# One order for two plans, later index copies and products of ones in an attention and expert kernel

## The chip, the cores and the metric

The kernel runs on one core of a Trainium2 chip. The metric is the time of one execution on the device in microseconds (us), as the median of the timed runs. A profile is one more execution, with its own time.

## The reference

Attention without a softmax, normalised per head, and then a mixture of experts with one expert per token:

```
kv  = einsum('bhsd,bhse->bhde', k, v)          # 8 batches, 8 heads, 576 tokens, 64
out = einsum('bhsd,bhde->bhse', q, kv)
x   = out / sqrt(mean(out*out) + 1e-6) * g_norm    # to [4608, 512]
e   = argmax(x @ w_gate);  p = softmax probability of e
# each of 8 experts keeps its first 1152 tokens, in order
y   = relu(x_e @ w1[e]) @ w2[e]                # 512 -> 1024 -> 512
result[token] = p * y   (0 for a token that was not kept)
```

All inputs are float32. The kernel splits float32 operands of the expert products into a high and a low float16 part and adds three products (high by high, high by low, low by high).

## The kernel before

**Attention.** Eight batches, each loaded in halves of four heads (k, v, q), through rings of three buffers that SyncE's queue fills. Of a batch, TensorE multiplies k by v, turns q (transposes by an identity, `turn` in `unit`, line 793) and multiplies turned q by kv (`product`, 818). VectorE and ScalarE copy results, make squares, a reciprocal root and the logits. `route` (866) makes of the logits the chosen expert, and of counts (products with a triangle of ones, L991) each token's place with its expert. `enter` (1028) adds ten small products per batch into one PSUM tile, `tab`: the table of tokens by expert and slot, complete after the last batch. The normalised rows go to a DRAM buffer `x_dram` from GpSimd's queue (L1050, L1052).

**Early expert.** After batch 2 the expert with the most tokens so far is picked, its weights are loaded and split, and after batch 4 its first 384 tokens are gathered and worked on within the attention part: first products in PSUM tiles named `op`, and the first of three row tiles of the second products also in `op`.

**Tables.** `finish` (1304) is the end of the first plan: it reads `tab` (L1112), cuts the row indices of the early expert's remaining rows, and ranks the experts (L1072 to L1108).

**Rounds.** The rest of the early expert (its row tiles 1 and 2 in PSUM tiles named `yp`; the rows from 384 to 704: round 0), then seven experts in order of their counts, with 672 to 544 rows each. For each round: weights are loaded in quarters (L341), VectorE takes maxima (`am`, L357), a scale is made through two small TensorE products (L370, L377) and a chain of small VectorE operations (`scale`, 379), ScalarE makes the high part (L391) and VectorE the low part (L397, tiles `w1l` and `w2l`). Rows are gathered by GpSimd (`xg`, L453), multiplied by the norm (`xm`), split and turned. Round 0's three row tiles are turned by TensorE (L472); later rounds' by transposing DMAs. First products are at L557 (`hp`), second ones at L604 and L613 (`yp`).

**Index copies.** `slots` (663) reads an expert's place in the table into a register and copies six columns of two tables (L669): a register load and two small copies. `rows_beside` (1588) calls it for each of the seven later rounds, and the gathers of that round use the copy. Its only dependency is the ranking.

**What sets the order.** A `Plan` (90) holds every step with its engines, an assumed length, dependencies and a key. `place` puts steps on engines by those lengths, the one that can start first, and among several that can start, the smallest key; no actual time enters. `emit` then writes out all steps by planned start. There are two plans: the first for attention, early expert and `finish`, the second for the rest. Each is written out within a region of its own, `tc.manual_schedule`, in which an engine keeps the order in which its instructions were written. Between the regions the pools of the attention part are closed.

Of the kernel before, what the change touches and what calls it, by code (L numbers as in the profile page):

```python
# [26 lines left out]
MANUAL = ("PE", "Activation", "DVE", "Pool", "SP")  # L27
# [17 lines left out]
FIRST = -50.0  # L45
KEY = 10.0
EARLY_TILES = 1
ROWS = 0.0
# [13 lines left out]
ON_X = 0  # L62

TARDY = (3.0, 3.0, 3.0, 3.0, 1.5, 3.0, 2.0, 0.5)
LATE = (4.0, 2.0, 1.0, 2.0)


# [22 lines left out]
class Plan:  # L90
# [5 lines left out]
    def op(self, ways, fn, deps=(), key=0.0, takes=(), uses=()):  # L96

        ways = [ways] if isinstance(ways[0], str) else list(ways)
        o = Op(ways, fn, [d for d in deps if d is not None], list(takes), key)
        for h in takes + uses if isinstance(takes, tuple) and isinstance(uses, tuple) else list(takes) + list(uses):  # L100
            h.users.append(o)
        self.ops.append(o)
        return o
# [56 lines left out]
def attention_moe_kernel(  # L160
# [12 lines left out]
    nc = tc.nc  # L173
# [4 lines left out]
    P = 128  # L178
# [507 lines left out]
    nc.vector.memset(warm, 0.0)  # L686
    nc.scalar.activation(warm, warm, AF.Exp)

    o_sbs, sss = [], []
    for i in range(NO):  # L690
        o_sbs.append(at.tile([P, C, H, XW], F32, name=f"o_sb{i}", bufs=1))
# [3 lines left out]
    op = plan.op  # L695
# [97 lines left out]
    def unit(b, n, ts, kv, ready, oh):  # L793
        key = b * C + n * C / len(UNITS)
        o_sb, kv2 = oh.t, kv.t.rearrange("p h f x -> p (h f) x")
        qp, qt = new("qp"), new("qt")
        half, u = UNITS[n]
        qh, qd = ts["q", half]
        m = 2 * len(BLOCKS[u]) * P

        def turn(e):
            qp.t = bank("qp")
            for w, t in enumerate(BLOCKS[u]):
                for p in range(2):
                    nc.tensor.transpose(qp.t[:, (2 * w + p) * P:(2 * w + p + 1) * P],
                                        qh.flat[:, (t + C * p) * P:(t + C * p + 1) * P], ident)

        def keep(e):
            qt.t = at.tile([P, 512], F32, name="qt", bufs=3)
            copy(e, qt.t[:, 0:m], qp.t[:, 0:m])  # L810

        o = op(("T", m / 980), turn, [qd], key - 1.2, (qp,), (qh,))
        kept = op([("A", 0.48), ("V", 0.6)] if m == 512 else [("A", 0.29), ("V", 0.34)], keep, [o], key - 1, (qt,), (qp,))
        done = []
        for w, t in enumerate(BLOCKS[u]):
            ph = new("op")

            def product(e, w=w, t=t, ph=ph):
                ph.t = bank("op")
                for p in range(2):  # L820
                    f = 2 * (half * HH + 2 * p + (t > 2))
                    x = kv2[:, f:f + 4:3] if t == 2 else kv2[:, f:f + 2]
                    nc.tensor.matmul(ph.t[:, p * 2 * XW:(p + 1) * 2 * XW], lhsT=qt.t[:, (2 * w + p) * P:(2 * w + p + 1) * P],  # L823
                                     rhs=x, start=True, stop=True)

            o = op(("T", 0.55), product, [kept] + ready, key, (ph,), (qt, kv))
            for s0, s1 in ((0, 1), (1, 2)) if t == 2 else ((0, 2),):

                def out_(e, t=t, ph=ph, s0=s0, s1=s1):
                    m0 = 2 * t + s0  # L830
                    h0, c0 = half * HH + m0 // C, m0 % C
                    copy(e, o_sb[:, c0:c0 + s1 - s0, h0:h0 + 3:2].rearrange("p c h x -> p h c x"),
                         ph.t[:, 0:4 * XW].rearrange("p (h c x) -> p h c x", h=2, c=2)[:, :, s0:s1])

                a = op([("A", 0.29), ("V", 0.37)] if s1 - s0 == 2 else [("A", 0.2), ("V", 0.22)], out_, [o], key, (oh,), (ph,))
                done += [((2 * t + i) % C, a) for i in range(s0, s1)]
        return done
# [28 lines left out]
    def route(b, oh, ssh, outs, sums):  # L866
# [159 lines left out]
                                 in1=tok_hl[:, :, cs].rearrange("p i (o c) -> p i o c", o=1).broadcast_to(s4), op=ALU.mult)  # L1026

        def enter(e):
            for c in range(C):
                for i in range(2):  # L1030
                    nc.tensor.matmul(tab[:, 0:W], lhsT=z["ohl"][:, :, c], rhs=z["rhs"][:, i, :, c],
                                     start=(b == 0 and c == 0 and i == 0), stop=(b == NB - 1 and c == C - 1 and i == 1),
                                     skip_group_check=True)
# [84 lines left out]
    def early_weights():  # L1118

        cnt = sm.tile([P, E], F32, name="cnt")  # L1120
        o = count(cnt, (PICK_AFTER + 1) * C)
        o = op(("V", 1.7), lambda e: pick(cnt), [o], (PICK_AFTER + 1) * C)

        def reg(e):
            early["reg"] = nc.sync.value_load(first_i[0:1, 0:1], min_val=0, max_val=E - 1)

        early["picked"] = [o]
        reg = op(("S", 0.05), reg, [o], W1_KEY)
        free = [[], [], [], []]
        for i, key in ((0, W1_KEY), (1, W2_KEY)):  # L1130
            loads = [op(("S", 0.43), lambda e, i=i, p=p: load_weight(i, early["reg"], raw1, p, 4),
                        [reg] + free[p], key) for p in range(4)]
            waits.append((loads, WAFTER[i]))
            loads = [op(("D", 1.46), None, [o]) for o in loads]
            for o in loads:
                o.late = LATE[3]
            f, z = split_weight(i, wsets[0], raw1)
            tops = []
            for p in range(4):
                key = WKEYS[i][0] + 2 * p * WKEYS[i][1]  # L1140
                if TOPS[i][p] == "A":
                    tops += [op(("A", 0.63), lambda e, f=f, p=p: f["sum"](p), [loads[p // 2]], key)
                             for p in (2 * p, 2 * p + 1)]
                else:
                    tops += [op(("V", 0.61), lambda e, f=f, p=p: f["top"](p), [loads[p // 2]], key)
                             for p in (2 * p, 2 * p + 1)]
            key = WKEYS[i][0] + 8 * WKEYS[i][1]
            o = op(("V", 0.3), lambda e, f=f: f["most"](), tops, key)
            o = op(("T", 0.12), lambda e, f=f: f["across"](misc[:, 128:256]), [o], FIRST)
            o = op(("V", 0.2), lambda e, f=f: f["across_max"](misc[:, 128:256]), [o], FIRST)  # L1150
            o = op(("T", 0.35), lambda e, f=f: f["back"](misc[:, 96:97]), [o], FIRST)
            o = op(("V", 1.1), lambda e, f=f: f["scale"](misc[:, 96:97]), [o], FIRST)
            free, highs, lows = [list(tops[2 * p:2 * p + 2]) for p in range(4)], {}, {}
            for n, p in enumerate((0, 2, 4, 6, 1, 3, 5, 7) if i == 0 else range(8)):
                after = key + n * WKEYS[i][1]
                highs[p] = a = op(HIGHS, lambda e, f=f, p=p: f["high"](p, e), [o], after)
                lows[p] = c = op(LOWS, lambda e, f=f, p=p: f["low"](p, e), [a], after)
                free[p // 2] += [a, c]
            early["free"] = free
            early["w", i], early["z", i] = (highs, lows), z  # L1160
# [180 lines left out]
    order = ExitStack()  # L1341
    order.enter_context(tc.manual_schedule(engines={getattr(mybir.EngineType, e) for e in MANUAL}))
    plan.emit()
    order.close()
    actx.close()


# [187 lines left out]
    def weights(r, key, after):  # L1535

        ws, sets, zs, holds = wsets[r % 2], [], [], []
        for i in range(2):
# [35 lines left out]
            o.late = LATE[2] if r > 1 else 0.0  # L1574
            o = op(("T", 0.31), lambda e, f=f, x=x: f["back"](x.t[:, 0:1]), [o], FIRST, (), (x,))
            ew = new(f"e{i}")
            o = op(("V", 1.1), lambda e, f=f, x=x: f["scale"](x.t[:, 0:1]), [o], FIRST, (ew,), (x,))
            zs.append((z, o, ew))
            highs, lows = [], []
            for p in range(8):  # L1580
# [4 lines left out]
            holds.append(hold)  # L1585
        return sets, zs, holds

    def rows_beside(r, key):

        hold, sl, st = new("xs"), new("slots"), {}  # L1590

        def cut(e):
            st["gi"], st["si"] = slots(mo, perm_i[0:1, 1, r:r + 1])

        cut_ = op(("V", 0.4), cut, [early["rank"]], key, (sl,))
        n = len(spans(0, BUDGET[r]))
        gates, turned, first, sent = [], [], None, []
        for i in range(n):
# [23 lines left out]
    def products(r, x, xh, xl, gates, xs_hold, si, sl_hold, sets, zs, w_holds, s0, s1):  # L1622
# [32 lines left out]
        def scales(e):  # L1655
            st["g2"] = Gemm2(mo, wsets[r % 2], st["g1"], x().gt, si(), s0, s1)
            st["g2"].scales(y_scale(*[z["e"] for z, _, _ in zs]))

        scaled = op(("V", 1.2), scales, hh[:1] + gates + [o for _, o, _ in zs], urgent, (),
                    (xs_hold, *[x for _, _, x in zs]))  # L1660
        second(r, st, hh, hl, sets and sets[1], scaled, hid, w_holds[1], sl_hold, s0, s1, y_bank)
        return hh
# [5 lines left out]
    def moved(e):  # L1668
# [6 lines left out]
                                              mo, None, lambda: psx.tile([P, 512], F32, tag="x", name="xp"), new("xs"), BM)  # L1675
    args = (lambda st=st: st["rows"], xh, xl, gates, xs_hold, lambda: early["si0"], Hold(None), None, zs, w_holds, EARLY,
            BUDGET[0])
    for r in range(E):
        hh = products(r, *args)
        key = KEY * r  # L1680
        if r + 1 < E:
            sets, zs, w_holds = weights(r + 1, key + 1, [] if r > 1 else sent)
            st, xs_hold, sl, gates, turned, sent = rows_beside(r + 1, key + ROWS)
            args = (lambda st=st: st["x"], turned, turned, gates, xs_hold, lambda st=st: st["si"], sl, sets, zs, w_holds, 0,
                    BUDGET[r + 1])
        else:
            op(("P", 9.0), lambda e: nc.gpsimd.drain(), hh[:2], key)
            steps, o = plan_rest(), hh[0]
            for _ in range(60):
                o = op(("V", 0.2), lambda e: next(steps, None), [o], key + 1)  # L1690
    order = ExitStack()
    order.enter_context(tc.manual_schedule(engines={getattr(mybir.EngineType, e) for e in MANUAL}))
    plan.emit()
    order.close()
    rest(**table)
# [31 lines left out]
```

## Time and profile before

| | |
|---|---|
| timed runs, median of 3 | 574.98 us (573.97 to 575.07) |
| profiled execution | 569.37 us |
| its span, first to last instruction | 567.6 us |
| TensorE (PE) busy | 528.5 us, 93% of the span |
| VectorE (DVE) busy | 386.8 us, 68% |
| ScalarE (ACT) busy | 252.6 us, 45% |
| GpSimd (POOL) busy | 198.9 us, 35% |
| mean granted TensorE clock | 0.982 of 2.4 GHz |

An instruction's row has its start in us from the span's start, its length, engine, line, operation, written tile <- read tiles, shapes, the count of merged instructions, and in brackets the idle time of its engine just before it with what ended that. "issue" is idle time for which the profile shows no releaser. PEld is TensorE's weight load. The granted clock is a share of 2.4 GHz: 1.00 is that level, 0.50 is 1.2 GHz.

### The profile page before, as it was taken

Reading aid. Unit: us, or ns where it says so; the run is one execution under the profiler, and the core shown is the slowest. Engines: PE = TensorE matmul, PEld = TensorE weight load, DVE = VectorE, ACT = ScalarE, POOL = GpSimd, SP = SyncE. Lnnn points to the kernel's source line nnn. Section 1 sums busy time; section 2 is a strip of 40 time slices with the busy share of each in tenths; the row PEclk is TensorE's granted clock in tenths of the full one; section 3 lists DMA queues with packets and bytes.
Section 4 is the critical chain, followed back from the end, with each engine's and each line's share of the span. In section 5 each row is a group of like instructions: output and inputs, shape, how many; then the busy total and the mean of one; then the engine's idle time right before and its main releaser. Section 6 shows DMA issues by size and latency. Waiting matters only on the chain.

```text
span 567.6 us, 11867 instructions
## 1 busy us (share of the span) xinstructions
PE 528.5 (93%) x4490; PEld 364.6 (64%) x4490; DVE 386.8 (68%) x1072; ACT 252.6 (45%) x490; POOL 198.9 (35%) x244
## 2 busy tenths in 40 slices
PE   4999987978877999999999999999999999999995
PEld 4988876965434576546754674677477558648843
DVE  4387897999838999998999677395848607203800
ACT  1687663886102662655625524253353426212201
POOL 3003335245132471355506431742452375021011
PEclk9999995999999999999999999999999999999998
DMA  8999999662149589699667565583665342010000
GB/s 279 332 357 357 377 383 381 210 257 95 52 150 360 113 250 261 154 308 180 198 160 239 163 153 164 143 172 101 206 159 122 79 102 57 18 55 22 2 37 33
DMA packets 81905, 102.71 MB, mean 181 GB/s; under 512 B 39148, under 2 KB 63724, under 8 KB 80818
## 3 DMA queue, kind: packets, MB, share of 16 engines
q1 hardware_dynamic: 74240, 70.50, 43.3%
q0 software_dynamic: 7584, 31.38, 16.7%
q8 instruction: 37, 0.61, 0.4%
q14 instruction: 26, 0.21, 0.1%
q10 hardware_dynamic: 18, 0.02, 0.0%
HBM read 73.20 MB, written 20.68 MB: 165 GB/s over the span
## 4 chain that ended last, share of the span: by engine, by line
issue 32%; PE 29%; DMA 16%; POOL 13%; DVE 8%; ACT 1%; POOLq 1%; SPq 0%; DVEq 0%
PE hp L557 10%; PE yp L604 9%; DMA v_sb<-in_v_dram 4%; POOL out_dram L634 4%; DMA k_sb<-in_k_dram 4%; POOL pair L490 4%; DMA q_sb<-in_q_dram 3%; POOL xg L453 3%; PE op L823 2%; POOL xm L461 2%; DMA xs<-pair 2%; DVE w1l L397 2%; PE op L557 2%; DMA raw<-in_moe_w_dram 2%; DMA xg<-x_dram,gi 1%
## 5 line engine op out<-in xcount | busy, mean ns | idle before, releaser
L557 PE MATMUL hp<-xs,w1h 128*128 128x320 f16 (+6 forms) x960 | 134.2, 292 | 2.4 <-DVE gt L466 1.2
L557 PEld LDWEIGHTS <-w1h 128*128 128x128 f16 x1024 | 99.4, 98 | 40.0 <-issue 7.3
L634 POOL DMA_INDIRECT out_dram<-ysb,si x42 | 42.9, 1020 | 153.8 <-ACT ysb L629 150.7
L604 PEld LDWEIGHTS <-hh 128*128 128x128 f16 x560 | 54.4, 98 | 63.7 <-issue 1.6
L562 ACT ACTIVATE hh<-hp 128x320 f16<-128x320 f32 (+7 forms) x64 | 41.0, 640 | 108.5 <-PE hp L557 108.5
L357 DVE TENSOR_REDUCE am<-raw 128x1 f32<-128x512 f32 x120 | 75.6, 673 | 4.1 <-DMA raw<-in_moe_w_dram 4.1
L629 ACT ACTIVATE ysb<-yp,ysc 128x512 f32<-128x512 f32 (+5 forms) x41 | 28.1, 685 | 99.9 <-PE yp L604 93.6
L557 PE MATMUL hp<-xs,w1l 128*128 128x320 f16 (+6 forms) x480 | 72.0, 292 | 0.0
L565 DVE SCALAR_TENSOR_TENSOR hl<-hp,hh 128x320 f16<-128x320 f32 (+7 forms) x64 | 47.4, 741 | 32.8 <-ACT hh L562 32.7
L604 PE MATMUL yp<-w2h,hh 128*128 128x512 f16 x272 | 65.3, 379 | 0.8 <-ACT ysb L629 0.8
L604 PE MATMUL yp<-w2l,hh 128*128 128x512 f16 x272 | 65.4, 383 | 0.0
L604 PE MATMUL yp<-w2h,hl 128*128 128x512 f16 x272 | 65.0, 381 | 0.0
L453 POOL DMA_INDIRECT xg<-x_dram,gi x42 | 44.0, 1048 | 49.6 <-DVE gt L466 13.0
L557 PEld LDWEIGHTS <-w1l 128*128 128x128 f16 x512 | 49.8, 98 | 16.3
L823 PE MATMUL op<-kv_bd,qt 128*128 128x144 f32 x320 | 53.0, 301 | 3.5 <-ACT qt L703 2.7
L397 DVE SCALAR_TENSOR_TENSOR w2l<-raw,sw,w2h 128x512 f16<-128x512 f32 x64 | 51.6, 848 | 5.2 <-ACT w2h L391 5.2
L619 DVE COPY yt<-yp 128x256 f32<-128x256 f32 (+4 forms) x7 | 2.9, 412 | 73.4 <-PE yp L613 63.8
L490 POOL TENSOR_TENSOR pair<-xm,pair 128x512 f16<-128x512 f32 (+5 forms) x26 | 34.0, 1308 | 50.3 <-ACT pair L486 50.1
L397 DVE SCALAR_TENSOR_TENSOR w1l<-raw,sg,w1h 128x512 f16<-128x512 f32 x64 | 50.1, 816 | 1.5 <-ACT w1h L391 1.5
L604 PEld LDWEIGHTS <-hl 128*128 128x128 f16 x280 | 27.3, 98 | 32.2 <-issue 1.1
L823 PEld LDWEIGHTS op<-kv_bd,qt 128*128 128x128 f32 x320 | 44.1, 196 | 5.6 <-ACT qt L703 2.9
L391 ACT ACTIVATE w2h<-raw,sw 128x512 f16<-128x512 f32 x62 | 39.7, 710 | 8.1 <-PE yp L613 7.2
(247 smaller groups left out, 698.0 us busy)
## 6 DMA issues: line engine op xcount, KB each, us to landing
raw<-in_moe_w_dram SPq DMA_DIRECT2D x64, 512.0 KB, 5.4
x_dram<-o_sb POOLq DMA_DIRECT2D x8, 720.0 KB, 6.5
k_sb<-in_k_dram SPq DMA_DIRECT2D x16, 320.0 KB, 6.6
v_sb<-in_v_dram SPq DMA_DIRECT2D x16, 320.0 KB, 7.9
q_sb<-in_q_dram SPq DMA_DIRECT2D x16, 320.0 KB, 6.9
x_dram<-o_sb POOLq DMA_DIRECT2D x8, 576.0 KB, 7.4
k_sb<-in_k_dram SPq DMA_DIRECT2D x16, 256.0 KB
v_sb<-in_v_dram SPq DMA_DIRECT2D x16, 256.0 KB, 4.5
```

The costliest lines, as they stand in the source:

```text
L357: nc.vector.tensor_reduce(out=am()[:, p:p + 1], in_=raw[:, sl(p)], axis=AX.X, op=ALU.max, apply_absolute_value=True)
L391: nc.scalar.activation(wh[:, sl(p)], raw[:, sl(p)], AF.Copy, scale=z["s"])
L397: nc.vector.scalar_tensor_tensor(out=wl[:, sl(p)], in0=raw[:, sl(p)], scalar=z["s"], in1=wh[:, sl(p)], op0=ALU.mult, op1=ALU.subtract)
L453: nc.gpsimd.indirect_dma_start(out=self.xg[i][0:n], out_offset=None, in_=x_dram[0:self.rows, :], in_offset=bass.IndirectOffsetOnAxis(ap=se ...
L490: eng.tensor_tensor(out=pair[0:n, 1], in0=self.xm[i][0:n], in1=pair[0:n, 0], op=ALU.subtract)
L557: nc.tensor.matmul(self.view(hp)[:, v], lhsT=w[:, c, f * P:(f + 1) * P], rhs=x[:, c, u * hw:(u + 1) * hw], start=(t == 0 and c == 0), stop ...
L562: nc.scalar.activation(self.out(self.hh, j), self.view(hp), AF.Relu)
L565: nc.vector.scalar_tensor_tensor(out=self.out(self.hl, j), in0=self.view(hp), scalar=0.0, in1=self.out(self.hh, j), op0=ALU.max, op1=ALU.s ...
L604: nc.tensor.matmul(yp[0:n, 0:DM], lhsT=h[:, j, o:o + n], rhs=w[:, j, :], start=(m == 0), stop=(m == len(self.terms) - 1))
L629: nc.scalar.activation(self.ysb[0:n], yp[0:n, 0:DM], AF.Copy, scale=self.ysc[0:n, i:i + 1])
L634: nc.gpsimd.indirect_dma_start(out=(disjoint.pop() if disjoint else out)[:, :], out_offset=bass.IndirectOffsetOnAxis(ap=self.sidx[0:n, col ...
L823: nc.tensor.matmul(ph.t[:, p * 2 * XW:(p + 1) * 2 * XW], lhsT=qt.t[:, (2 * w + p) * P:(2 * w + p + 1) * P], rhs=x, start=True, stop=True)
```

## The change

A helper `busy` issues products of a matrix of ones with itself, 256 columns each, into an unused part of the PSUM tile `misc`; their results are not read. It is called ahead of one turn of batch 3 (6 products), one of batch 4 (24), both the first turn of q's second half, and ahead of the first product of batch 7 (10). The other places where it could be called have zero. The planned lengths don't count it.

The first region is no longer closed after the first plan: both plans are written out in one. In the second plan, index copies for the rounds from the second on also depend on the last low part of round 0's rows. Three assumed lengths grow: an index copy from 0.4 to 0.9, `scale` from 1.1 to 1.4 in weights of the rounds from the second on, and `scales` (the output scale) from 1.2 to 2.4 in the rounds from the first on.

```diff
+BUSY_TURNS = {(3, 1): 0.7, (4, 1): 2.6}
+BUSY_PRODUCTS = {(7, 0, 0): 1.1}
+BUSY_ENTERS = {}
+BUSY_SCALES = (0.0, 0.0)
...
+    def busy(us, dst=None):
+        dst = misc if dst is None else dst
+        for _ in range(round(us / 0.109)):
+            nc.tensor.matmul(dst[:, 256:512], lhsT=ones16, rhs=ones16.rearrange("p (o x) -> p o x", o=1).broadcast_to([P, 2, P]),
+                             start=True, stop=True)
...
         def turn(e):
+            busy(BUSY_TURNS.get((b, n), 0.0))
             qp.t = bank("qp")
...
             def product(e, w=w, t=t, ph=ph):
+                busy(BUSY_PRODUCTS.get((b, n, w), 0.0))
                 ph.t = bank("op")
...
     plan.emit()
-    order.close()
     actx.close()
...
-            o = op(("V", 1.1), lambda e, f=f, x=x: f["scale"](x.t[:, 0:1]), [o], FIRST, (ew,), (x,))
+            o = op(("V", 1.4 if r > 1 else 1.1), lambda e, f=f, x=x: f["scale"](x.t[:, 0:1]), [o], FIRST, (ew,), (x,))
...
-    def rows_beside(r, key):
+    def rows_beside(r, key, after=()):
...
-        cut_ = op(("V", 0.4), cut, [early["rank"]], key, (sl,))
+        cut_ = op(("V", 0.9), cut, [early["rank"], *after], key, (sl,))
...
-        scaled = op(("V", 1.2), scales, hh[:1] + gates + [o for _, o, _ in zs], urgent, (),
+        scaled = op(("V", 2.4 if r > 0 else 1.2), scales, hh[:1] + gates + [o for _, o, _ in zs], urgent, (),
...
+    placed = xl[-1:]
     for r in range(E):
...
-            st, xs_hold, sl, gates, turned, sent = rows_beside(r + 1, key + ROWS)
+            st, xs_hold, sl, gates, turned, sent = rows_beside(r + 1, key + ROWS, placed if r else ())
...
-    order = ExitStack()
-    order.enter_context(tc.manual_schedule(engines={getattr(mybir.EngineType, e) for e in MANUAL}))
     plan.emit()
     order.close()
```

## Rows read from the trace of the kernel before

**Rows 1.** The page's part 1: engine, busy us, share of the span, instructions.
```profile
PE 528.5 (93%) x4490; PEld 364.6 (64%) x4490; DVE 386.8 (68%) x1072; ACT 252.6 (45%) x490; POOL 198.9 (35%) x244
```

**Rows 2.** Waits of PE from 185 us on: total us, times, longest.
```profile
PE hp L557 <- DVE gt L466: 1.2, 1, 1.2
```

**Rows 3.** Sums by stretch: length, busy PE PEld DVE ACT POOL, clock, DMA share, GB/s.
```profile
92.70:99.60 6.90, 6.82 (x47) 6.74 (x48) 3.69 (x15) 4.24 (x10) 4.13 (x4) 0.51 1.10 374
98.00:150.00 52.00, 45.06 (x410) 35.55 (x409) 50.20 (x159) 36.26 (x91) 18.20 (x26) 0.99 0.46 164
154.50:176.50 22.00, 14.36 (x72) 7.16 (x71) 10.05 (x42) 3.61 (x6) 7.79 (x8) 0.92 0.65 229
158.50:159.00 0.50, 0.50 (x4) 0.21 (x3) 0.00 (x0) 0.00 (x0) 0.00 (x0) 1.00 0.06 25
167.70:171.20 3.50, 3.47 (x11) 1.79 (x12) 1.69 (x9) 0.59 (x1) 1.17 (x2) 0.51 0.91 267
176.50:204.50 28.00, 27.57 (x244) 17.35 (x244) 27.16 (x73) 16.76 (x31) 13.73 (x13) 1.00 0.70 199
```

**Rows 4.** Timeline of PE, then of DVE, around the join of the plans.
```profile
155.32 1.89 PE L604 MATMUL yp<-w2h,hh 128*128 128x512 f16 x8 [0.78 <-ACT ysb L629]
159.85 0.75 PE L1031 MATMUL tab<-rhs,ohl 128*128 128x48 f16 x10
...
155.39 0.46 DVE L1024 TENSOR_TENSOR rhs<-ohh,tok_hl 128x480 f16<-128x480 f16 x1
160.63 0.27 DVE L1112 SCALAR_TENSOR_TENSOR tab_sb<-slot_pos,cap,tab 128x48 f32<-128x48 f32 x1 [4.78 <-PE tab L1031]
166.93 0.69 DVE L461 TENSOR_TENSOR xm<-xg 128x512 f32<-128x512 f32 x1 [2.29 <-issue]
167.54 0.26 DVE L1108 TENSOR_REDUCE bud_e<-cmp 128x8 f32<-128x64 f32 x1
```

**Rows 5.** The chain that ended last: start, us, what.
```profile
165.65 6.38 DMA xg<-x_dram,gi
...
174.83 0.68 DVE xm L461
```

**Rows 6.** Timeline of DVE from the second tile on, and PE's first product.
```profile
168.69 0.17 DVE L669 COPY gi<-gidx_tab 128x6 int32 x1 [0.60 <-issue]
...
172.06 0.15 DVE L466 TENSOR_SCALAR gt<-xg 64x1 f32<-64x1 f32 x1 [0.27 <-DMA xg<-x_dram,gi]
172.82 0.17 DVE L669 COPY gi<-gidx_tab 128x6 int32 x1 [0.62 <-issue]
...
174.61 0.17 DVE L669 COPY gi<-gidx_tab 128x6 int32 x1 [0.60 <-issue]
...
176.48 1.76 PE L557 MATMUL hp<-xs,w1h 128*128 128x320 f16 x11 [0.46 <-ACT xs L703]
```

**Rows 7.** Timeline of POOL and SP: the first gather, and round 1's weights.
```profile
163.06 1.03 POOL L453 DMA_INDIRECT xg<-x_dram,gi  x1 [6.27 <-DVE cmp L1096]
164.93 5.97 SPq L341 DMA_DIRECT2D raw<-in_moe_w_dram  x8
```

**Rows 8.** Timeline: DVE's last low part of round 1's w1, PE's first use.
```profile
204.16 0.73 DVE L397 SCALAR_TENSOR_TENSOR w1l<-raw,sg,w1h 128x512 f16<-128x512 f32 x1
206.86 1.30 PE L557 MATMUL hp<-xs,w1l 128*128 128x336 f16 x8
```

**Rows 9.** Timeline of PE and DVE in the attention part.
```profile
70.31 0.66 PE L805 MATMUL qp<-ident,q_sb 128*128 128x128 f32 x4
86.50 2.40 PE L739 MATMUL a<-v_sb,k_sb 128*64 128x64 f32 x40 [2.79 <-DMA v_sb<-in_v_dram]
89.77 0.37 PE L370 MATMUL misc<-ident,a 128*1 128x128 f32 x1 [0.87 <-DVE a L367]
92.78 1.08 PE L805 MATMUL qp<-ident,q_sb 128*128 128x128 f32 x4 [1.64 <-DMA q_sb<-in_q_dram]
94.81 0.18 DVE L705 COPY kv_bd<-a 64x32 f32<-64x32 f32 x1 [2.03 <-ACT kv_bd L703]
117.48 1.25 PE L823 MATMUL op<-kv_bd,qt 128*128 128x144 f32 x8 [2.66 <-ACT qt L703]
```

More of the change, by code (lines that the diff above doesn't have):

```diff
@@ L1028, in enter @@
         def enter(e):
+            busy(BUSY_ENTERS.get(b, 0.0))
             for c in range(C):
@@ L1148, in early_weights @@
             o = op(("V", 0.3), lambda e, f=f: f["most"](), tops, key)
-            o = op(("T", 0.12), lambda e, f=f: f["across"](misc[:, 128:256]), [o], FIRST)
+            o = op(("T", 0.12), lambda e, f=f, i=i: (busy(BUSY_SCALES[0] * (i == 0)), f["across"](misc[:, 128:256])), [o], FIRST)
             o = op(("V", 0.2), lambda e, f=f: f["across_max"](misc[:, 128:256]), [o], FIRST)
-            o = op(("T", 0.35), lambda e, f=f: f["back"](misc[:, 96:97]), [o], FIRST)
+            o = op(("T", 0.35), lambda e, f=f, i=i: (busy(BUSY_SCALES[1] * (i == 0)), f["back"](misc[:, 96:97])), [o], FIRST)
             o = op(("V", 1.1), lambda e, f=f: f["scale"](misc[:, 96:97]), [o], FIRST)
```

## The prediction

> **What bounds the kernel now.** I read the page's first part, then the waits of TensorE (PE), then sums by stretch, then the chain of work that ended last, and last the order of time around the join of the two plans. The reader should see this. PE is busy for 93% of the span [rows 1], and the idle time lies ahead of 185 us: from there to the end the longest PE wait is 1.2 us, once [rows 2], so the expert rounds are a solid train of matmuls. What makes PE begin that train earlier moves the end by the same amount, unless a stall comes back behind it. VectorE (DVE) is nearly as full as PE from 98 to 150 us (50.20 of 52 us) and again from 176.5 to 204.5 us (27.16 of 28) [rows 3]; there PE can gain nothing that DVE doesn't.
>
> Between 154.5 and 176.5 us PE is idle for 22 - 14.36 = 7.6 us [rows 3], and that hole has one story. The last table product (L1031) starts on PE at 159.85 us, but its last input, rhs, was written by DVE from 155.39 to 155.85 us [rows 4]. In between stand the products of the early expert's second row tile (tile yp, which only the second plan makes): instructions of the second plan ran ahead of the last PE instruction of the first. DVE does the same (xm of the second plan at 166.93 us, then bud_e, the last of the first plan [rows 4]). So with two regions the order written out holds within a region, not across the join. DVE sits idle for 4.78 us before tab_sb [rows 4], which leads to the row indices, the gathers on POOL [rows 7], the third gather's landing (6.38 us in the chain [rows 5]), xm of the third tile, and the first product of round 0 at 176.48 us [rows 6].
>
> **The change part by part.**
>
> *One region.* The order is then that of the program: the table product before any yp. It can start when rhs is there, 155.85 us, with about 0.1 us to pass on the signal: 155.95 instead of 159.85, so 3.9 us earlier. It is followed by the same DVE work, so the first gather could be issued at 163.06 - 3.9 = 159.16 us [rows 7]. A second bound: the gathers read what the last batch wrote to x_dram, and those bytes stop in the slice 158.5 to 159 us (25 GB/s left [rows 3]); with a signal of up to 0.9 us behind the bytes the gather may wait until 159.5. I take 3.8 us for the chain; bounds 3.5 and 3.9. The cost: PE waits for rhs where it had begun yp at 155.32 us, some 0.6 us. It isn't on the path: behind the table PE has 48 yp products, 8 of them in at most 1.89 us [rows 4], so at most 11.3 us, and three short turns, and is done near 169 us, before the third tile is ready (170.0, below). The weights of round 1 are issued at 164.93 us, behind the same DVE chain [rows 7], and come earlier with it, so that gathers and weights meet as before. If the region changed nothing, this term is 0. An instruction that used to run ahead of the join could also have helped; the only two shown are yp, which costs the 0.6 us counted, and xm, which waited for its gather anyhow.
>
> *Later index copies.* Each copy of indices for a round is a register load and two small copies, 0.90 us apart (172.82 to 174.61 us holds two such steps) [rows 6]. Five of them stand in the hole, for rounds 1 to 5; the first stays, the other four wait for the last low half of round 0's rows. Three of them stand between the landing of the third tile (gt at 172.06, done 172.21) and its xm at 174.83 us [rows 5, 6]: 2.6 us on the path, which go. Nothing else is late there: PE and ScalarE follow xm by 176.48 - 174.83 = 1.65 us as before. The copy at 168.69 us lies in a wait for a gather, and going saves nothing.
>
> Together round 0 starts 3.8 + 2.6 = 6.4 us earlier, at 170.1 us.
>
> *Where the copies go.* Four times 0.90 = 3.6 us of DVE work move into a stretch where DVE has 28 - 27.16 = 0.84 us free [rows 3]. Queued behind them are the splits of round 1's weights. The last w1l is done at 204.89 us and PE first wants one at 206.86 us [rows 8], so 2.0 us are in hand. All four there: 3.6 - 0.84 - 2.0 = 0.8 us of stall; none there: 0. Against it, round 1's weights are issued only 3.8 us earlier while the products start 6.4 earlier, 2.6 us less lead, which could add as much. From 0 to 3.4 us, then; I take 0.6, near the low end, because a copy has the lowest rank among what is ready and goes to gaps.
>
> *Longer planned lengths (0.9 for a copy, 1.4 for a scale, 2.4 for scaled).* No instruction comes or goes; the order of the second plan on all engines may. The only stall that a better order could take away is the 1.2 us [rows 2], and a worse one can make such stalls. I take 0; bounds: 1.2 us gained, and 1.2 us lost at the start of each of the seven later rounds (8.4 us; the rival below).
>
> *Products of ones.* 6, 24 and 10 matmuls of 256 columns. No such row is there; by eight of 512 columns in 1.89 us [rows 4] one is at most 1.89 / 8 / 2 = 0.12 us: 0.7, 2.8 and 1.2 us. They wait for nothing new: the bank that they write was last read well before. The ten stand ahead of the last batch's first product, where PE waits 2.66 us for ScalarE [rows 9]; hidden, and 1.2 us if that wait went. The other 30 stand where PE is busy, in batches 3 and 4 (the turn at 70.31 us), and push PE back by 3.5 us. Up to 2.8 of these fall into the wait for v at 86.50 us, which is set by the transfers (DMA share 1.10 still from 92.7 to 99.6 us [rows 3]); with the earlier waits for DVE nearly all is hidden on PE. DVE lives on PE's results there and comes 3 us later too, until its own wait of 2.03 us at 94.81 us [rows 9] takes up most of it. The clock: it was granted at 0.51, the 1.2 GHz level, from 92.7 to 99.6 us [rows 3], after PE had waited 2.79 us [rows 9]. Filling that wait can keep it at 2.4 GHz for a while, but then the wait at 89.77 us, for DVE, grows: DVE's value comes about 3 us later and v's products are done sooner, so PE stands from about 88 to 92 us, longer than the wait that dropped the clock before. I take 0.2 us lost for all forty; bounds: 4.7 us lost (nothing hidden) and 1.8 us gained, since from 98 us DVE has only 52 - 50.20 = 1.8 us to give [rows 3].
>
> The Trainium skill ("TensorE: Matmul & The Clock Gate", Part 1) says that the throttled clock is the default and that activity releases it; no run here shows the default by itself. By that rule the added activity pays back the whole slow stretch: half of 6.9 us, 3.4 us on PE. The trace has PE wait for DVE behind it, so the sum goes by 1.8 at most.
>
> **Sum.** 3.8 + 2.6 - 0.6 + 0 - 0.2 = 5.6 us. The profiled execution took 569.37 us (567.6 of span and 1.8 around it) and would take 563.8. The median of the timed runs is 574.98, 5.6 us above it; I take the difference to stay: 574.98 - 5.6 = 569.4 us.
>
> **Rivals.**
>
> *The clock holds.* PE keeps 2.4 GHz through 86 to 100 us and DVE passes on all of its 1.8 us: 2.0 better than the sum, 567.4 us. For: the waits before 86 us are filled. Against: the wait for DVE grows.
>
> *The order was not the region's doing.* The table product stays behind yp for another reason (say, a bank that it must wait for), and only the copies go: 574.98 - 2.6 + 0.2 = 572.6 us. For: nothing in the profile names what put yp first. Against: two engines show second-plan work ahead of first-plan work at the join, and neither does within a plan.
>
> *DVE takes it back.* The copies and the shorter lead of the weights cost their upper bound, 3.4 in place of 0.6: 572.2 us.
>
> *Late rows at each round's start, slower.* The copy for a round now stands in a DVE queue that is full, the round's gathers wait for it on POOL, and PE meets at the start of each of the seven later rounds what it meets once now, 1.2 us for rows not yet there [rows 2]: 8.4 us lost against 6.2 gained (the sum without its 0.6), 577.2 us. It decides from 6.2 / 7 = 0.9 us per round. For: DVE has no room where these copies go [rows 3] and the planned order is new. Against: the copies need not be that late; each round's rows are gathered a round ahead.
>
> **How the numbers follow.** The forecast 0.62 (own range 568 to 571), the clock 0.11, the order 0.08, DVE 0.08, late rows 0.08; the remaining 0.03 lies near no change. Runs of this kernel differ by 1.1 us, 0.2%, which is what can be told from no change: faster means under 573.8. With the upper parts of the order and DVE cases near that line: faster 0.84, same 0.07, slower 0.09. The range holds the forecast, the clock and most of the two cases at 572: 566.0 to 573.4.
>
> **What would show it.** Right: PE's last table product directly behind rhs and ahead of all yp; tab_sb near 157 us, the third tile's xm right behind its gt, the first hp of round 0 near 170 us, and no second stretch at the lower clock like that near 168 to 171 us [rows 3]. Copies 0.90 us apart further back among the weight splits. The forty products as one row of 128x256, the 24 followed by a v wait under 0.5 us, and a longer wait at the next product for DVE's value. Wrong: yp still ahead of the table; round 1's first w1l product waiting for DVE by over 2 us; PE waits above 1 us at several round starts; the attention part ending over 1 us later than 154.5 us.

## The result, and the profile after

The changed kernel takes 567.14 us (565.97 to 567.73, 4 runs); the kernel before took 574.96 us beside it (573.97 to 575.07, 4 runs). The ratio is 0.9865 with an interval of 0.9845 to 0.9885: 7.8 us faster, where 5.6 were forecast. A later comparison gave 562.63 against 570.86 us, a ratio of 0.9854 (0.9823 to 0.9884), 8.2 us. It is called the repeat below; its profile is of the same changed kernel. One run of e6, at 571.58 us, was counted as slow and is left out of the numbers of e6.

The profiled execution after took 565.97 us, with a span of 564.1 us. PE is busy for 94% of it, against 93% [rows 1]:

```profile
PE 532.7 (94%) x4530; PEld 368.5 (65%) x4530; DVE 390.9 (69%) x1071; ACT 252.3 (45%) x490; POOL 201.4 (36%) x245
```

The same stretches as in [rows 3]:

```profile
92.70:99.60 6.90, 6.90 (x49) 6.79 (x49) 5.11 (x24) 4.28 (x10) 4.31 (x4) 0.52 1.03 365
98.00:150.00 52.00, 45.06 (x404) 36.17 (x403) 47.88 (x153) 35.78 (x90) 18.01 (x26) 0.95 0.43 155
154.50:176.50 22.00, 19.44 (x121) 10.40 (x120) 14.46 (x58) 4.57 (x9) 10.10 (x11) 1.00 0.71 258
167.70:171.20 3.50, 2.99 (x17) 1.37 (x14) 1.80 (x5) 1.11 (x2) 0.78 (x2) 1.00 0.87 299
176.50:204.50 28.00, 27.05 (x241) 16.94 (x240) 26.42 (x65) 15.96 (x29) 13.87 (x12) 1.00 0.81 192
```

The hole is the third row: PE is idle for 2.6 of the 22 us, before for 7.6. The stretch at the lower clock (fourth row, clock 0.51 before) is gone. The timeline of PE and DVE at the join, which answers [rows 4] and [rows 6]:

```profile
158.80 0.74 PE L1045 MATMUL tab<-rhs,ohl 128*128 128x48 f16 x10 [1.36 <-DVE rhs L1037]
159.36 1.91 PE L608 MATMUL yp<-w2h,hh 128*128 128x512 f16 x8
...
172.57 1.90 PE L561 MATMUL hp<-xs,w1h 128*128 128x320 f16 x12 [0.46 <-ACT ysb L633]
...
158.28 0.46 DVE L1037 TENSOR_TENSOR rhs<-ohh,tok_hl 128x480 f16<-128x480 f16 x1
159.58 0.27 DVE L1126 SCALAR_TENSOR_TENSOR tab_sb<-slot_pos,cap,tab 128x48 f32<-128x48 f32 x1 [0.83 <-issue]
...
170.77 0.15 DVE L470 TENSOR_SCALAR gt<-xg 64x1 f32<-64x1 f32 x1 [0.16 <-DMA xg<-x_dram,gi]
170.85 0.75 DVE L465 TENSOR_TENSOR xm<-xg 64x512 f32<-64x512 f32 x1
174.83 0.15 DVE L673 COPY gi<-gidx_tab 128x6 int32 x1
```

The table product is right behind rhs and ahead of yp, the third xm right behind its gt, and the next index copy comes 4 us later. But rhs itself ends at 158.74 us, 2.9 us later than before. The reason stands at 112 us, on ScalarE and then on PE:

```profile
112.64 0.37 ACT L714 COPY kvs<-a 128x256 f32<-128x256 f32 x1 [3.23 <-remote]
...
113.06 0.69 PE L774 MATMUL a<-ident,kvs 128*128 128x128 f32 x2 [2.10 <-ACT kvs L714]
```

"remote" means that the event which ended the wait has no sender in the trace. The profiled execution before has no such wait, nor has the repeat. All five profiles of the first two comparisons (the changed kernel and experiments e1 to e4) have the wait, at 3.2 to 3.4 us, and none of the eight of the later two, so it does not go with the change. It may go with the chip: the last three comparisons ran on three different ones; which chip the first ran on is not known. Two experiments have the attention part of before unchanged (e2 and e3), and there rhs ends at 159.4 and 159.2 us, later than in the profile after. Such a wait would explain most of why the timed runs of before lay 5.6 us above its profiled execution; as those runs left no profile, this is likely and not shown.

It also means that executions should be compared by stage. Each row is one profiled execution: the end of the last rhs, the start of round 0's first hp, the time between, and from there to the end of the span.

| kernel | rhs ends | first hp | join | rounds |
|---|---|---|---|---|
| before | 155.85 | 176.48 | 20.6 | 391.1 |
| after | 158.74 | 172.57 | 13.8 | 391.5 |
| the repeat (e10) | 157.24 | 171.23 | 14.0 | 389.6 |
| e1, no ones | 158.17 | 172.88 | 14.7 | 391.7 |
| e2, region alone | 159.43 | 179.00 | 19.6 | 394.1 |
| e3, copies alone | 159.23 | 177.43 | 18.2 | 395.2 |
| e4, ones alone | 159.08 | 179.71 | 20.6 | 393.2 |
| e5, all but the region | 155.73 | 173.93 | 18.2 | 389.4 |
| e6, all but the lengths | 155.61 | 169.86 | 14.3 | 398.4 |
| e13, all but the scales' lengths | 155.78 | 169.66 | 13.9 | 393.5 |
| e8, small ScalarE work more | 155.66 | 169.36 | 13.7 | 391.5 |
| e9, ones also in a wait | 155.87 | 169.14 | 13.3 | 394.2 |
| e11, the same kernel as e9 | 156.61 | 170.53 | 13.9 | 389.5 |
| e12, ones moved into a wait | 155.94 | 169.89 | 13.9 | 389.2 |

The repeat and the profile of before are alike in having no wait at kvs. There the attention part loses 1.4 us, the join gains 6.6 and the rounds gain 1.5; the sum is 6.7, and so far apart are their times, 569.37 and 562.65 us. Single executions of one kernel differ in a stage by as much as the two small terms: the rounds of e9 and e11, one kernel, take 394.2 and 389.5 us.

### The profile page after: what moved, and what is told of

It reads as the page before. It is cut to its first block, busy times and chain, and to the rows that moved or that the text cites. A ratio compares the mean times of both kernels' runs of the same rounds, so it can differ in the third digit from the quotient of the medians.

```text
span 564.1 us, 11943 instructions
## 1 busy us (share of the span) xinstructions
PE 532.7 (94%) x4530; PEld 368.5 (65%) x4530; DVE 390.9 (69%) x1071; ACT 252.3 (45%) x490; POOL 201.4 (36%) x245
## 4 chain that ended last, share of the span: by engine, by line
PE 39%; issue 30%; POOL 11%; DVE 11%; DMA 4%; ACT 2%; another core or an unknown queue 1%; POOLq 0%; SPq 0%; ACTq 0%
PE yp L608 13%; PE hp L561 12%; POOL out_dram L638 4%; PE op L836 4%; POOL pair L494 3%; DMA k_sb<-in_k_dram 2%; PE a L750 2%; PE qp L817 2%; POOL xm L465 2%; POOL xg L457 2%; DVE am L361 2%; PE op L561 2%; DMA q_sb<-in_q_dram 1%; DVE w2l L401 1%; PE yp L617 1%
## 5 line engine op out<-in xcount | busy, mean ns | idle before, releaser
L561 PEld LDWEIGHTS <-w1h 128*128 128x128 f16 x1024 | 99.6, 98 | 37.9 <-issue 5.3
L401 DVE SCALAR_TENSOR_TENSOR w2l<-raw,sw,w2h 128x512 f16<-128x512 f32 x64 | 53.5, 873 | 2.6 <-ACT w2h L395 2.6
L401 DVE SCALAR_TENSOR_TENSOR w1l<-raw,sg,w1h 128x512 f16<-128x512 f32 x64 | 51.9, 847 | 0.7 <-ACT w1h L395 0.7
L465 POOL TENSOR_TENSOR xm<-xg 128x512 f32<-128x512 f32 (+5 forms) x33 | 39.4, 1194 | 18.2 <-DVE pair L494 14.1
```

What stands on the lines that cost most here:

```text
L401: nc.vector.scalar_tensor_tensor(out=wl[:, sl(p)], in0=raw[:, sl(p)], scalar=z["s"], in1=wh[:, sl(p)], op0=ALU.mult, op1=ALU.subtract)
L465: eng.tensor_tensor(out=self.xm[i][0:n].rearrange("p (h d) -> p h d", h=H), in0=xg[:, :, 0:D], in1=xg[:, :, D:D + 1].broadcast_to([n, H, D ...
L561: nc.tensor.matmul(self.view(hp)[:, v], lhsT=w[:, c, f * P:(f + 1) * P], rhs=x[:, c, u * hw:(u + 1) * hw], start=(t == 0 and c == 0), stop ...
```

## The experiments

There were four comparisons, each with its own runs of the kernel before: after alone (before 574.96 us); e1 to e4 (573.79); e5, e6, e8 and e9 (570.05); e10 to e13 (570.86).

**e1: the changed kernel without the ones.**

```diff
-BUSY_TURNS = {(3, 1): 0.7, (4, 1): 2.6}
-BUSY_PRODUCTS = {(7, 0, 0): 1.1}
+BUSY_TURNS = {}
+BUSY_PRODUCTS = {}
```

> The changed kernel without the forty products of ones; all else as changed. Theory A (the sum on record): the ones are worth about nothing, so this stays within 0.5 us of the changed kernel's 567.1 us, about 7.8 us under the kernel before; one region and the index copies carry the gain. Theory B (the 2.2 us by which the gain exceeds the sum are the ones' doing, by the clock they hold): 569.3 us, 5.6 under the kernel before.

Measured: 566.8 us, ratio 0.9887 (0.9844 to 0.9929). Nearer to theory A: 7.0 us by the medians are there without the ones. Theory B's 569.3 us would be a ratio of 0.990, which lies within the interval; what speaks against it is e4.

**e2: one region alone.**

```diff
     plan.emit()
-    order.close()
     actx.close()
...
-    order = ExitStack()
-    order.enter_context(tc.manual_schedule(engines={getattr(mybir.EngineType, e) for e in MANUAL}))
     plan.emit()
```

> The kernel before with one region for both plans and nothing else. Theory A: the table product comes right behind rhs, ahead of all yp; 3.8 us gained (3.5 to 3.9), 571.2 us; the three index copies still stand between the third tile's gt and its xm. Rival (the order was not the region's doing): 575 us, yp still ahead of the table product.

Measured: 572.51 us (568.98 to 577.24), ratio 0.9969 (0.9935 to 1.0003): 1.8 us by the ratio, less than 3.8, and its interval just includes no change. The time alone does not separate the theories; the order does, and came out as theory A has it:

```profile
159.48 0.75 PE L1031 MATMUL tab<-rhs,ohl 128*128 128x48 f16 x10 [1.36 <-DVE rhs L1024]
160.06 1.91 PE L604 MATMUL yp<-w2h,hh 128*128 128x512 f16 x8
...
161.66 0.17 DVE L669 COPY gi<-gidx_tab 128x6 int32 x1 [0.56 <-issue]
...
164.51 1.02 POOL L453 DMA_INDIRECT xg<-x_dram,gi  x1 [4.15 <-DVE cmp L1107]
...
174.34 0.15 DVE L466 TENSOR_SCALAR gt<-xg 64x1 f32<-64x1 f32 x1 [2.09 <-DMA xg<-x_dram,gi]
...
177.11 0.68 DVE L461 TENSOR_TENSOR xm<-xg 64x512 f32<-64x512 f32 x1
```

The index is ready at 161.83 us, but the gather starts at 164.51, 2.7 us later; in the kernel before it starts 0.87 us behind its index (162.19 and 163.06). cmp, which the row names as releaser, had just ended and is no input of the gather; the write of x_dram is. By the semaphore's reports in the trace its last part is done at 163.38 us, while the fifteen before it came by 161.59, so the gather is 1.8 us late, and so is that part. The stretches around it show what one late part of sixteen looks like in the DMA columns:

```profile
161.50:162.00 0.50, 0.50 (x4) 0.20 (x2) 0.34 (x3) 0.00 (x0) 0.00 (x0) 1.00 0.81 315
162.00:162.50 0.50, 0.50 (x4) 0.25 (x3) 0.40 (x3) 0.00 (x0) 0.00 (x0) 1.00 0.05 18
162.50:163.00 0.50, 0.50 (x4) 0.24 (x3) 0.45 (x2) 0.00 (x0) 0.00 (x0) 1.00 0.06 27
```

The last report of that write is 1.12 or 1.13 us ahead of the first gather in e1, e2, e6, after and the repeat (163.38 and 164.51 here, 160.94 and 162.06 after), and 4.2 us ahead of it in the kernel before. From the end of rhs to the first gather it takes 7.2 us before, 3.3 after and 5.1 here. With the table early, this write is the next bound on the gathers, and it can lie further out than the 3.5 us allowed for. The profiled execution, 574.89 us, is among the slower ones of a wide spread; six of the twelve runs, at 568.98 to 571.62, lie 2.2 to 4.8 us under the median before and fit the 3.8. Whether the other six all had such a late part is not shown. The copies still cost 2.8 us between gt and xm, as expected. The profile lost time in round 0 too, at a granted clock of 0.50 from 176.2 to 183.0 us: the first twelve products, 1.90 us in the profile after, take 3.36.

```profile
179.00 3.36 PE L557 MATMUL hp<-xs,w1h 128*128 128x320 f16 x12 [0.46 <-issue]
```

**e3: later copies alone.**

```diff
-    def rows_beside(r, key):
+    def rows_beside(r, key, after=()):
...
-        cut_ = op(("V", 0.4), cut, [early["rank"]], key, (sl,))
+        cut_ = op(("V", 0.4), cut, [early["rank"], *after], key, (sl,))
...
+    placed = xl[-1:]
...
-            st, xs_hold, sl, gates, turned, sent = rows_beside(r + 1, key + ROWS)
+            st, xs_hold, sl, gates, turned, sent = rows_beside(r + 1, key + ROWS, placed if r else ())
```

> The kernel before with later index copies alone (the new dependency; the planned length stays 0.4), in two regions. Theory A: the third xm stands right behind its gt, 2.6 us gained, less up to 0.6 for crowding: 572.4 to 573.0 us. Rival (the copies crowd VectorE in round 0 by their upper bound of 3.4 us): 575.8 us, with a wait for w1l at the first products of round 1.

Measured: 574.63 us, ratio 1.0002 (0.9978 to 1.0027): nothing. Both theories are half right. The join is 18.2 us, 2.4 less than before, and xm follows gt:

```profile
175.59 0.15 DVE L466 TENSOR_SCALAR gt<-xg 64x1 f32<-64x1 f32 x1 [0.18 <-DMA xg<-x_dram,gi]
175.67 0.68 DVE L461 TENSOR_TENSOR xm<-xg 64x512 f32<-64x512 f32 x1
```

But the rounds take 395.2 us, against 391.1 in the profile of before. No wait for w1l of 3.4 us took the gain back. PE's waits in the rounds are mostly small ones, 4.3 us in all against 1.5 before. That is 2.8 of the 4.1 us by which these rounds are longer than before's; the rest is not traced. Of the yp waits, e4 has 0.8 us and the profile after 1.6, so not all are the copies' doing:

```profile
PE yp L613 <- issue: 2.3, 7, 0.5
PE hp L557 <- DVE gt L466: 1.2, 1, 1.2
PE hp L557 <- DVE hl L565: 0.8, 2, 0.6
```

**e4: the ones alone.** The kernel before with `busy` and its calls from the diff.

> The kernel before with the forty products of ones alone. Theory A: 0.2 us lost, within 0.5 us of the kernel before (575 us); the wait for v shorter, the wait for VectorE behind it longer, the granted clock falling there all the same. Theory B (the clock holds and the whole 2.2 us come from here): 572.8 us.

Measured: 574.88 us, ratio 1.0012 (0.9987 to 1.0037): theory A; theory B's 572.8 us would be a ratio of 0.996, outside the interval. The 24 hide in the wait for v, and the next wait, for DVE's a, is longer than the 0.87 us of [rows 9]:

```profile
69.97 2.79 PE L697 MATMUL misc<-ones 128*128 128x256 f16 x24
...
85.73 1.39 PE L750 MATMUL a<-v_sb,k_sb 128*64 128x64 f32 x40
...
91.88 0.37 PE L374 MATMUL misc<-ident,a 128*1 128x128 f32 x1 [4.77 <-DVE a L371]
```

**e5: the changed kernel with two regions.**

```diff
     plan.emit()
+    order.close()
     actx.close()
...
+    order = ExitStack()
+    order.enter_context(tc.manual_schedule(engines={getattr(mybir.EngineType, e) for e in MANUAL}))
     plan.emit()
```

> The changed kernel with the two regions back (copies, lengths and ones as changed). Theory A (the sum on record): the region is worth 3.8 us, 570.9 us; the table product stands behind yp again, some 4 us behind rhs. Rival (one region is worth what it was worth alone, 1.3 us of 573.8): 568.4 us.

Measured: 565.98 us, ratio 0.9929 (0.9904 to 0.9954), 4.1 us under the kernel before. The changed kernel's ratio makes 562.4 of this comparison's 570.05, so the region is worth 3.6 us beside the other edits. The tab product is 4 us behind rhs again, at 159.73, and the join 18.2 us against 13.8 to 14.0. Theory A.

**e6: the changed kernel with the lengths of before.**

```diff
-        cut_ = op(("V", 0.9), cut, [early["rank"], *after], key, (sl,))
+        cut_ = op(("V", 0.4), cut, [early["rank"], *after], key, (sl,))
...
-            o = op(("V", 1.4 if r > 1 else 1.1), lambda e, f=f, x=x: f["scale"](x.t[:, 0:1]), [o], FIRST, (ew,), (x,))
+            o = op(("V", 1.1), lambda e, f=f, x=x: f["scale"](x.t[:, 0:1]), [o], FIRST, (ew,), (x,))
...
-        scaled = op(("V", 2.4 if r > 0 else 1.2), scales, hh[:1] + gates + [o for _, o, _ in zs], urgent, (),
+        scaled = op(("V", 1.2), scales, hh[:1] + gates + [o for _, o, _ in zs], urgent, (),
```

> The changed kernel with the planned lengths of before (0.4 for a copy, 1.1 and 1.2 for the scales). Theory A (the sum on record): the lengths are worth nothing, 567.1 us within 0.5. Theory C (the copies put late without their length crowd VectorE, as the rounds of the copies-alone kernel say: 395.2 us from the first hp to the end against 391.5 in the changed kernel): 3.7 us slower, 570.8 us, with waits of PE near 205 to 207, at 287 and of 1.2 us near 425 us.

Measured: 567.44 us (562.9 to 570.63), ratio 0.995 (0.9923 to 0.9978). Against 562.4 by the changed kernel's ratio it is 5.1 us slower. Theory A, the sum on record, falls. The join is as good as after (14.3 us), and the rounds take 398.4. The waits of PE in the rounds, and the largest of them on DVE and on PE:

```profile
PE yp L628 <- DVE yt L623: 3.8, 1, 3.8
PE pt_max L381 <- DVE bm L378: 1.4, 1, 1.4
PE hp L561 <- DVE gt L470: 1.2, 1, 1.2
PE hp L561 <- DVE hl L569: 0.3, 1, 0.3
...
258.32 1.28 DVE L361 TENSOR_REDUCE am<-raw 128x1 f32<-128x512 f32 x2 [1.55 <-DMA raw<-in_moe_w_dram]
261.68 0.69 DVE L361 TENSOR_REDUCE am<-raw 128x1 f32<-128x512 f32 x1 [2.08 <-DMA raw<-in_moe_w_dram]
...
263.30 0.29 DVE L623 COPY yt<-yp 128x128 f32<-128x128 f32 x1
263.74 1.01 PE L628 MATMUL yp<-ident,yt 128*32 128x128 f32 x4 [3.76 <-DVE yt L623]
```

DVE takes its work in the order written out. It stands 2.08 us for a quarter of the next weights to land; yt, which is behind it, would have been ready (the last product into its yp ended at 254.84 us), and PE waits for yt. A granted clock of 0.50 follows, from 262.5 to 269.4 us. The runs spread over 562.9 to 570.6 us; that the landing of the weights differs with them is likely, but one execution alone was profiled.

The longer lengths do not rule such a stall out. The profiled execution of e9 below, which has them, took 565.18 us, its other six runs 560.06 to 561.49; in it DVE stands 3.19 us for weights and PE 2.57 us behind it, and the clock is at 0.50 from 298.1 to 301.6 us:

```profile
293.26 1.28 DVE L361 TENSOR_REDUCE am<-raw 128x1 f32<-128x512 f32 x2 [3.19 <-DMA raw<-in_moe_w_dram]
...
296.49 0.38 PE L381 MATMUL pt_max<-bm,ones 1*128 1x1 f32 x2 [2.57 <-DVE bm L378]
```

By the times it is likely rarer with them: the changed kernel's own runs lie within 1.8 us of each other, those of e6 within 7.7.

**e8: 24 small instructions more on ScalarE.**

```diff
     nc.scalar.activation(warm, warm, AF.Exp)
+    for _ in range(24):
+        nc.scalar.activation(warm, warm, AF.Abs)
```

> The changed kernel with 24 tiny instructions more on ScalarE in its idle time before 14 us; they compute nothing that is used. It asks what the 3.2 us are for which ScalarE stands ahead of kvs at 112.6 us in the changed kernel, with the last event it waited for long past. Theory D (ScalarE waits there for its own instructions, moved in pieces of a fixed number; 24 more shift the place): the wait at kvs is gone, comes elsewhere, and the attention part ends up to 3 us earlier, 564 to 566 us. Theory E (it waits for data or for a transfer): nothing changes, 567.1 us, the wait at kvs stays.

Measured: 561.6 us, ratio 0.9845 (0.982 to 0.987), as the changed kernel by ratio. It decides nothing: in this comparison no kernel had the wait at kvs, the others without the 24 neither.

**e9 and e11: forty ones more in the wait for DVE's a.** The same kernel twice.

```diff
-BUSY_SCALES = (0.0, 0.0)
+BUSY_SCALES = (4.4, 0.0)
```

> The changed kernel with forty more products of ones on PE ahead of the transposing product at 91.4 us, where PE stands 4.76 us for VectorE's a; 40 of 0.109 us are 4.4 us and fill that wait. Theory A (the sum on record): the clock then stays at 2.4 GHz up to 99 us, but VectorE sets the pace, which has at most 1.8 us to give: 565.3 to 567.1 us. Theory B (the slow stretch costs what it costs PE, half of its 6.9 us): 563.7 us.

> The changed kernel with forty more products of ones in the wait ahead of the transposing product, as before, now beside the changed kernel. Theory A (VectorE sets the pace from 86 to 100 us): within 1 us of the changed kernel, although the clock stays at 2.4 GHz there. Theory B (the slow stretch costs half of its length on PE): 3.4 us faster than the changed kernel.

Measured: 560.62 us, ratio 0.9833 (0.9808 to 0.9857), and 561.18 us beside 562.63 of the changed kernel, ratio 0.9829 (0.9799 to 0.9859): 1.4 us better, and the intervals overlap. From 92.7 to 99.6 us, in the repeat, then in e11 and in e9:

```profile
92.70:99.60 6.90, 6.59 (x47) 6.16 (x48) 5.37 (x29) 3.51 (x9) 3.15 (x4) 0.59 1.04 358
```

```profile
92.70:99.60 6.90, 5.99 (x64) 5.32 (x62) 4.91 (x25) 4.04 (x11) 2.70 (x3) 1.00 0.91 302
```

```profile
92.70:99.60 6.90, 5.42 (x55) 4.72 (x53) 6.44 (x29) 5.25 (x13) 3.88 (x4) 1.00 1.04 359
```

The granted clock is at 2.4 GHz, and far less than 3.4 us comes out: nearer to theory A, though 1.4 is a little more than the 1 us that it allowed. In e9 the ones fit the wait, and DVE is busy for 6.44 of the 6.9 us while PE has time to spare: DVE's pace, as theory A has it. In e11 they outlast it. DVE's a is written by 91.73 us, the ones end at 94.08, and DVE stands for the product behind them, so there the ones themselves also hold DVE back:

```profile
89.11 4.97 PE L697 MATMUL misc<-ones 128*128 128x256 f16 x40
...
94.23 0.28 DVE L378 TENSOR_REDUCE bm<-misc 1x1 f32<-1x128 f32 x1 [1.91 <-PE misc L374]
```

**e10: the changed kernel once more.** No edit.

> The changed kernel itself once more, beside the kernel before on the chip of the next three kernels, so that it can be set against them. Theory A (the gain is the kernel's and not the chip's): a ratio of 0.984 to 0.989, about 8 us. Rival (part of the first gain was the chip's): the 3.4 us by which the two profiled executions differ, a ratio of 0.994.

Measured: 562.63 us, ratio 0.9854 (0.9823 to 0.9884). Theory A. PE's waits from 185 us on, which answer [rows 2]; the 1.2 us is down to 0.8 (in the profile after it is gone, and five waits ahead of yp, 1.6 us in all, stand in its place):

```profile
PE hp L561 <- DVE gt L470: 0.8, 1, 0.8
```

**e12: ones only where PE waits.** e9 without the thirty ahead of the two turns.

```diff
-BUSY_TURNS = {(3, 1): 0.7, (4, 1): 2.6}
+BUSY_TURNS = {}
...
-BUSY_SCALES = (0.0, 0.0)
+BUSY_SCALES = (4.4, 0.0)
```

> The same without the thirty products of ones ahead of the turns of batches 3 and 4: the ones in the wait ahead of the transposing product, and the ten of batch 7, stay. Theory A (the thirty cost and bring nothing, the wait for v takes them up): within 0.5 us of the kernel with both. Rival (they hold the clock into the wait): the granted clock falls near 86 us in the wait for v, and the time is 1 to 2 us longer.

Measured: 560.25 us (557.39 to 561.17), ratio 0.9804 (0.977 to 0.9838). The rival is half right: the clock falls at 83.3 us in the wait for v, and the time is not longer, but 0.9 us shorter. This version is 2.4 us under the changed kernel by the medians and 10.6 under the kernel before, the best median of all; the ratios' intervals overlap, the runs themselves (561.56 to 563.19 for the changed kernel) do not. Its ones are too many for the wait: DVE's a is written by 88.39 us, and DVE then stands for the product behind the ones.

```profile
93.47 0.28 DVE L378 TENSOR_REDUCE bm<-misc 1x1 f32<-1x128 f32 x1 [4.48 <-PE misc L374]
```

**e13: the copy's length alone.** The changed kernel with the two scales' lengths of before (the last two edits of e6).

> The changed kernel with the longer length for an index copy (0.9) but the scales' lengths of before (1.1 and 1.2). With all three as before it was 5.7 us slower than the changed kernel's ratio gives. Theory F (a copy planned at 0.4 that takes 0.9 shifts VectorE's order, the scales' lengths are worth nothing): as the changed kernel, within 0.7 us. Theory G (the scales' lengths set where the waits for weights stand on VectorE): 3 to 6 us slower than the changed kernel, with PE waits above 1 us between 200 and 310 us or near 430 us.

Measured: 565.66 us, ratio 0.9917 (0.989 to 0.9945), 3.0 us slower than the changed kernel: theory G at its lower edge. Of the 5.1 us of e6 (5.7 with the run that is left out here) some 3.0 are the scales' and 2.1 the copy's, across two comparisons and no surer than their intervals. PE's waits in the rounds, 4.1 us where the repeat has 0.8:

```profile
PE hp L561 <- DVE hl L569: 2.5, 3, 1.3
PE hp L561 <- DVE gt L470: 1.2, 1, 1.2
PE pt_max L381 <- DVE bm L378: 0.4, 1, 0.4
```

## Why the prediction was right, and where it was not

The time, 567.1, is within the range and 2.3 us under the forecast, below the forecast's own range of 568 to 571. It lies by the 567.4 us of the rival whose clock holds, but that mechanism is absent: the clock is at 0.52 from 92.7 to 99.6 us. The range reached down that far only for this rival, so that it holds the result is in part luck; what made up the difference is the step that failed, below.

**One region: right.** The order at the join is as described. The term was 3.8; e5 gives 3.6 by times and 18.2 - 13.9 = 4.3 by the join. The second bound of that step, the write of x_dram, was allowed 0.9 us behind its bytes and a gather at 159.5; the runs show 1.12 us from its last report to the gather, and a last part that can be late. What was not foreseen is that the region alone gives 1.8: in its profile that write decides, 1.8 us late, and round 0 starts at the lower clock; the other runs of e2 have no trace. PE's wait for rhs is 1.36 us where 0.6 was counted, off the path as described.

**Later copies, at the join: right.** The term was 2.6; the join of e3 is 2.4 us shorter. Both together were 6.4 and gave 6.6 (the repeat) and 6.8 (after).

**Where the copies go, 0.6 lost, and the longer lengths, 0: these steps failed,** and they are one step. I costed the copies by DVE's free time near round 1's first weights, and the lengths as an edit without instructions. The runs show that late copies with the old lengths give back all that they gain (e3: 2.4 us at the join, nothing in the time), and that the lengths are worth 5.1 us: without them the rest of the change gives 2.6 us by the medians of e6. In the repeat the two together shorten the rounds by 391.1 - 389.6 = 1.5 us where I had them lose 0.6, and e5, which lacks the region alone, says the same by its time: 4.1 us gained, of which the join has 2.4 and the rounds the other 1.7. That difference of some 2.1 us is nearly the 2.3 by which the forecast missed; the profile after, with rounds of 391.5 us, does not show it, so the attribution is likely rather than shown. The upper bound of 1.2 us, from the one wait [rows 2], was the nearer end; the 8.4 us on the other side is of the order of what e6 lost, but was worked out from late rows. The late-rows rival named the right queue: DVE's order in the rounds decides. In e6 it was maxima of late weights that stood ahead of a value for PE, not rows missing. The 2.0 us in hand for round 1's w1l were used up without a stall: the last one ends at 202.65 + 1.21 = 203.86 us in the profile after, and PE takes it at 204.04.

**The ones, 0.2 lost: right within what can be told.** e4 lost 0.7 us by the ratio and e1 gained nothing clear. The 24 are in one row of 2.79 us, the wait for v is gone, and the wait for a grew from 0.87 to 4.76 us:

```profile
69.48 2.79 PE L697 MATMUL misc<-ones 128*128 128x256 f16 x24
...
91.39 0.37 PE L374 MATMUL misc<-ident,a 128*1 128x128 f32 x1 [4.76 <-DVE a L371]
```

One sign for "wrong" did come true: the attention part ended over 1 us late. In the profile after, that is mainly the wait at kvs; in the repeat, which lacks it, it is 1.4 us. The ones are hardly the reason: of the six other profiles with the thirty and without that wait, five (e5, e6, e8, e9 and e13) end rhs at 155.6 to 155.9 us, as before and as e12 without the thirty (155.94), and e11 at 156.6. By time the thirty cost 0.9 us (e11 against e12), in runs that overlap.

The Trainium skill ("TensorE: Matmul & The Clock Gate", Part 1) has activity release the throttled clock. The traces of e9 and e11 agree (1.00 from 92.7 to 99.6 us, in place of 0.52 and 0.59 in the two profiles of the changed kernel). The time that this rule would give back, 3.4 us, did not come: in e9 DVE's pace kept most of it, in e11 also the ones that outlasted the wait.

**The difference between profile and median** was taken to stay at 5.6 us. It did not: after, it is 1.2 us. The gain of 7.8 is between medians, where this does not enter.

## What to carry to other kernels

An order that is written out from assumed lengths has those lengths as part of the kernel: an edit that moves work into a full engine is costed together with them, and lengths that are short by 0.3 to 1.2 us, in a queue that is full, cost some 5 us here. Gains at a join are read from stage to stage (last input to first product), as the executions differ elsewhere by more. Products that only hold the clock belong in a wait of TensorE, not ahead of one; they bring no more than the engine behind them can use, and take it back where they outlast the wait.

## What the runs showed that was not expected

In two of four comparisons ScalarE stood for 3.2 to 3.4 us ahead of the same copy, kvs near 112 us, in all five profiles, and in none of the eight of the other two; the medians of the kernel before were 575.0 and 573.8 us in the former, 570.1 and 570.9 in the latter. A packet of 8,192 bytes of instructions moved just then in both kinds of profile; whether ScalarE waited for it is open, since the test for it (e8) ran in a comparison without the wait.
